# A self-scheduled recurrence-and-MLP kernel: new step durations, a reordered weight conversion, and a buffer left free earlier

## The chip, the cores and the metric

The kernel runs on one core of a Trainium2 chip. The metric is the device time of one execution in microseconds (us). Before the change it is 795.39 us, the median of three runs (794.29 to 796.77). The profile used below is of an execution of 794.98 us, whose recorded span is 793.3 us.

The engines have short names here: PE is the matrix engine (PEld its weight loads), DVE the vector engine, ACT the scalar (activation) engine, POOL the GpSimd engine. SP is the sync engine, which only issues transfers. POOL issues transfers too.

## The reference

A gated linear recurrence over time with a complex gate, followed by a two-layer MLP with a squared ReLU. Sizes: 4 batches, 8 heads, 768 time steps, head dimension 48; the MLP is 384 to 2048 to 384 over 3072 rows. The two MLP weights come as 64-bit floats.

```python
def _attn_ref(q, k, v, a_re, a_im):
    mag = np.sqrt(a_re * a_re + a_im * a_im)
    scale = np.minimum(mag, 0.999) / (mag + 1e-06)
    a_re_n, a_im_n = (a_re * scale, a_im * scale)
    ...
    for t in range(S):
        new_re = ar * S_re - ai * S_im
        new_im = ar * S_im + ai * S_re
        S_re, S_im = (new_re + kv, new_im)          # kv: outer product of k[t] and v[t]
        y[:, :, t] = np.einsum('bhd,bhde->bhe', q[:, :, t], S_re)

def _moe_ref(x, w_in, w_out):                       # x: the y of all heads side by side
    h = x @ w_in
    r = np.maximum(h, 0.0)
    return ((r * r) @ w_out).astype(np.float32)
```

## The kernel before

The time axis is cut into halves of 384 steps, which gives 8 units n = 0 to 7 (4 batches, two halves). A unit goes through three parts:

1. **The chain**, on DVE and ACT, for two groups of four heads (z = 0, 1): load `a` (the gate), q, k and v; normalise the gate (steps `sq`, `m2`, `ln`, `ex`, `s2`, `r1`, `r2`, `n1`, `n2`, `l1`, `l2`); multiply three neighbouring time steps together (`in10` to `in23`); invert the product (`iq`, `ia`, `il`, `ie`, `i1`, `i2`); transpose the ends on PE (`tot`); run a prefix product over time in ten parts on DVE (`scan`, eight tiny instructions in a part); transpose back (`bk`, copied to `xn`). Then the products `f` of `a` and `xn` are combined and applied to q and k (`QK`).
2. **The attention of four head pairs**, on PE with evictions on ACT and DVE: transposes `tq`, scores `sa`, states `kv` (from `KC`, the keys sent through DRAM as `rows` and read back), the mix `ypair`, the copy `yt`, and a transfer into `xT`.
3. **The dense part**: 16 pieces of `h` (three matmuls each), ReLU and square on ACT, then 3 output blocks `o` of 16 matmuls. Both together are 96 matmul instructions of 384 columns; as each fp32 matmul shows as two records, they are 192 records.

Nothing is placed by hand. Each piece of work is a `step` with an engine, a duration (`cost`, ns), a latency to its result (`lag`), a rank and its dependencies. `lay_out` plays the steps through with these numbers, and the order in which they start there is the order in which each engine gets its instructions. The real engines then work through these fixed queues and wait, in order, on semaphores. So a number in `step` changes no instruction; it changes the order.

```python
def lay_out():
    ...
    while ready:
        # for each engine: the steps that can start earliest, by rank among those nearly as early
        picks = [min((p for p in ps if p[0] <= min(ps)[0] + NEARLY.get(engine, 0)), key=lambda p: p[1])
                 for engine, ps in picks.items()]
        t, _, key = min(picks)
        engine, cost, lag, _, _, _, bank, until = steps[key]
        free[engine] = t + cost
        done[key] = t + cost + lag
        ...
    return [(t, key) for t, _, key in sorted(starts)]
```

The weights: 32 pieces (16 of each matrix) are fetched as 64-bit words and turned into fp32 in one ACT pass (`lower`) and three DVE passes that depend on each other.

```python
def lower(i):
    act.activation(out=lo, in_=lo, func=AF.Copy, scale=2.0 ** -29)

def convert(i, part):
    if part == 0:
        dve.tensor_scalar(out=bits, in0=hi, ...)                     # L676
    elif part == 1:
        dve.scalar_tensor_tensor(out=bits, in0=hi, ..., in1=bits, ...)   # L679
    else:
        dve.tensor_tensor(out=bits, in0=bits, in1=more, op=ALU.add)  # L683
```

`rest` is a check on the size of the inputs: ACT squares a tile into a scrap tile `junk` and keeps only the sum, for q, k and v.

```python
def measure(j, t):
    act.activation(out=junk[:, 0:t.shape[1]], in_=t, func=AF.Square, saturate=False,
                   accum_out=sums[:, n, j:j + 1])
...
for i in range(3):
    add(("rest", n, i), "ACT", act_cost(2 * NEL) + 90,
        [("kk", n, i) if i < 2 else ("v", n, W - 1)],
        lambda i=i: measure(4 + i, whole(u["qk", i]) if i < 2 else v_of_the_unit))   # v: cut
```

The last stage of the chain. In units 0 and 1 the two products are joined by PE into PSUM (`join_pe`, tile `P`); from unit 2 on by DVE (`join`), which writes into `a`:

```python
def cross(z, j, r):
    dve.tensor_tensor(out=u["fb" if j else "fa", z][:, r], in0=u["a", z][:, r], in1=over(z, j), op=ALU.mult)

def join(z, r):
    a, fa, fb = u["a", z], u["fa", z], u["fb", z]
    dve.tensor_tensor(out=flat(a[:, r]), in0=flat(fa[:, r]), in1=flat(fb[:, 1 - r]),
                      op=ALU.add if r else ALU.subtract)

def apply(z, j, r, i=None):
    p = u["a", z][:, r] if i is None else u["P", z, r, i]
    dve.tensor_tensor(out=outs(z)[j][...], in0=u["qk", z][:, j, hi], in1=p, op=ALU.mult)
```

There is one buffer `a` for each z, so the next unit's load of `a` waits until the last reader of the present one is through.

Of the kernel before, what the change touches and what calls it, by code (L numbers as in the profile page):

```python
# [481 lines left out]
def fast_path(ctx, tc, q, k, v, a_re, a_im, moe_w_in, moe_w_out, out, flag):  # L482
# [10 lines left out]
    nc = tc.nc  # L493
# [5 lines left out]
    NP = H // 2  # L499
# [185 lines left out]
    def weight_steps():  # L685
        for i in range(2 * NF):
            if i < FIRST:
                deps = [("gate", z) for z in range(2)]
            elif i < NF:
                deps = [("cv", i - FIRST, 2)]  # L690
            else:
                deps = [("cv", i - (NF - NF // 2 if i < NF + NRAW else NRAW), 2)]
            step(("fetch", i), "SP" if i >= NF else "POOL", 100 if i >= NF else 750, 400 + i,
                 deps, lambda i=i: fetch(i), 7000)
            rank = CONV[i // NF] + i
            step(("lower", i), "ACT", 470, rank, [("fetch", i), ("e2", 0, 1)], lambda i=i: lower(i))
            for part, cost in enumerate((270, 470, 470)):
                step(("cv", i, part), "DVE", cost, rank,
                     [("cv", i, part - 1), ("lower", i) if part == 2 else ("fetch", i),
                      ("ap", 0, 1)],  # L700
                     lambda i=i, part=part: convert(i, part))
# [41 lines left out]
    def chain_steps(u):  # L743
        n = u["n"]
        NEL = HH * W * D
        count = [0]
        get, queue, issue = ((nc.sync, "SP", 100) if n < 2 else (nc.gpsimd, "POOL", 750))

# [22 lines left out]
        for name in ("a", "qk"):  # L771
            for z in range(2):
                for j in range(2):
                    add(("ld", n, name, z, j), queue, issue,
                        [("ap", n - 1, z)],
                        lambda name=name, z=z, j=j: load(name, z, j),
                        lag=(4300 + 2700 * z if name == "a" else 8000) if n == 0 else 6000)
        for j in range(W):
            add(("v", n, j), queue, issue,
                [("mix", n - 2, NP - 1), ("kv", n - 2, NP - 1), ("rest", n - 2, 2)],  # L780
                lambda j=j: load_v(j), lag=9000 if n < 2 else 6000)
        if n == 0:
# [239 lines left out]
        for i in range(3):  # L1022
            add(("rest", n, i), "ACT", act_cost(2 * NEL) + 90,
                [("kk", n, i) if i < 2 else ("v", n, W - 1)],
                lambda i=i: measure(4 + i, whole(u["qk", i]) if i < 2 else
                                    u["v"].rearrange("p j h d -> p (j h d)")))

# [40 lines left out]
        def join(z, r):  # L1068
            a, fa, fb = u["a", z], u["fa", z], u["fb", z]
            dve.tensor_tensor(out=flat(a[:, r]), in0=flat(fa[:, r]), in1=flat(fb[:, 1 - r]),  # L1070
                              op=ALU.add if r else ALU.subtract)
# [9 lines left out]
        def apply(z, j, r, i=None):  # L1081
            hi = slice(0, HH) if i is None else ts(i, HH // 2)
            p = u["a", z][:, r] if i is None else u["P", z, r, i]
            dve.tensor_tensor(out=outs(z)[j][:, hi, :, r * D:(r + 1) * D],  # L1084
                              in0=u["qk", z][:, j, hi], in1=p, op=ALU.mult)
# [15 lines left out]
        for z in range(2):  # L1101
# [10 lines left out]
            for r in range(2):  # L1112
# [10 lines left out]
                else:  # L1123
                    add(("join", n, z, r), "DVE", D1, made + [("f", n, z, 1, r), ("f", n, z, 0, 1 - r)],
                        lambda z=z, r=r: join(z, r))
# [19 lines left out]
    def pair_steps(u, i):  # L1145
# [107 lines left out]
        for h in range(2):  # L1253
            step(("sa", n, i, h), "PE", 650, rank + 3 + 3 * h,
                 [("T", n, i, c) for c in range(W)] + free, lambda h=h: score(h),
                 bank="sc", until=("A", n, i, h))
            step(("A", n, i, h), "DVE", 480, -20, [("sa", n, i, h)],
                 lambda h=h: scored(h))
        step(("kv", n, i), "PE", 165 * chunks, rank + 4,
             [("KC", n, z), ("v", n, W - 1), ("mix", n - 1, NP - 1)] + free, keep, bank=bank(True), until=("S", n, i, chunks - 1))  # L1260
        for j in range(chunks):
            step(("S", n, i, j), "DVE", 180, -21,
                 [("kv", n, i), ("S", n, i, j - 1)],
                 lambda j=j: kept(j))
        step(("mix", n, i), "PE", 1300 if late else 1100, rank + 12,
             [("A", n, i, h) for h in range(2)] + [("S", n, i, chunks - 1), was("y", 1)], mix)
        step(("y", n, i), "ACT", 400, -25, [("mix", n, i), was("xT", 2)], mixed)
        step(("xT", n, i), "SP", 200, -25, [("y", n, i), ("h", n - 2, NF - 1)], place, lag=2400)


    def dense_steps(u):
# [44 lines left out]
        for c in range(W):  # L1316
            for p in range(4):
# [103 lines left out]
```

## Time and profile before

| What | Value |
|---|---|
| time, median of 3 | 795.39 us |
| span of the profiled execution | 793.3 us |
| PE busy | 712.3 us, 90% |
| DVE busy | 509.7 us, 64% |
| ACT busy | 411.4 us, 52% |
| POOL busy | 107.1 us, 14% |
| dense matmuls, 1536 records of 487 to 496 ns | about 517 us of the PE time |
| mean granted PE clock | 0.979 |

A row of the wait table reads: engine, what waited (tile and line), what it waited for, then the total in us, how many times, and the longest. A row of the timeline reads: start in us, length in us, engine, line, operation, output and inputs, shape, number of instructions merged into the row, and in brackets the idle time ahead of it with what ended it. A row of the window table reads: the stretch in us, its length, the busy time of each engine in it (with its number of instructions), the PE clock as a share of full speed, the share of the transfer engines, and GB/s. Matmul records overlap, so a single record's length is more than the distance to the next: 24 dense records take 7.74 us on the chain of waits, 0.3225 us each, which is 0.645 us for one instruction.

### The profile page before, as it was taken

What the parts mean: (1) busy time and instruction counts of PE and PEld (TensorE: products, weight loads), DVE (VectorE), ACT (ScalarE), POOL (GpSimd) and SP (SyncE); (2) the same over time, 40 slices, a digit from 0 to 9 for tenths busy, and PEclk for the clock granted to TensorE, in tenths of its full rate; (3) what the DMA queues carried; (4) which work ended last, traced back from release to release, by engine and by line L of the source; (5) the groups of instructions that cost most, each with busy time, mean ns of one, the idle gap of its engine ahead of it and who ended that gap; (6) DMA issues with size and microseconds to landing.
All of it is one profiled execution on the core that took longest, in us unless ns stands there. A gap on an engine that the chain in (4) does not pass through costs nothing.

```text
span 793.3 us, 9897 instructions
## 1 busy us (share of the span) xinstructions
PE 712.3 (90%) x3538; PEld 474.7 (60%) x3538; DVE 509.7 (64%) x1184; ACT 411.4 (52%) x754; POOL 107.1 (14%) x157
## 2 busy tenths in 40 slices
PE   0139789989699999999999999999999999999996
PEld 0018645658466775776586668656865775555553
DVE  5498778886769679767966794698659536610000
ACT  5445359507493766775387538754775233502510
POOL 5001200004102210400121030103000204300000
PEclk9999789989899999999999999999999999999999
DMA  9406464007202520611161043105200518800000
GB/s 283 153 1 217 122 204 134 19 12 228 52 1 76 181 63 11 219 26 55 67 197 45 11 151 104 46 0 196 91 14 0 190 35 283 288 12 22 0 11 23
DMA packets 39068, 76.25 MB, mean 96 GB/s; under 512 B 10753, under 2 KB 25217, under 8 KB 39009
## 3 DMA queue, kind: packets, MB, share of 16 engines
q0 software_dynamic: 14208, 53.88, 21.1%
q1 hardware_dynamic: 24800, 21.64, 9.0%
q8 instruction: 30, 0.49, 0.3%
q14 instruction: 30, 0.24, 0.1%
HBM read 56.62 MB, written 14.16 MB: 89 GB/s over the span
## 4 chain that ended last, share of the span: by engine, by line
PE 68%; DVE 19%; ACT 4%; SPq 3%; DMA 3%; issue 2%; ACTq 0%; DVEq 0%
PE h L1277 24%; PE o L1294 22%; PE sa L1183 5%; PE tq L1170 5%; DVE fa L980 5%; PE kv L1197 4%; PE ypair L1219 3%; DVE e L987 2%; SPq L768 2%; PE ypair L1224 2%; PE P L1078 2%; ACT fa L806 2%; DVE qk L852 1%; DVE fa L985 1%; DMA xT<-yt 1%
## 5 line engine op out<-in xcount | busy, mean ns | idle before, releaser
L1277 PE MATMUL h<-xT,w 128*128 128x384 f32 x768 | 261.6, 496 | 8.5 <-DMA xT<-yt 8.4
L1294 PE MATMUL o<-w,g 128*128 128x384 f32 x768 | 255.5, 487 | 0.0
L1277 PEld LDWEIGHTS h<-xT,w 128*128 128x128 f32 x768 | 146.1, 194 | 106.5 <-issue 16.4
L1294 PEld LDWEIGHTS o<-w,g 128*128 128x128 f32 x768 | 143.0, 190 | 92.0 <-issue 0.6
L1175 ACT COPY QKT<-tq 96x512 f32<-96x512 f32 x96 | 76.3, 868 | 67.1 <-PE tq L1170 66.4
L1284 ACT ACTIVATE g<-h 128x384 f32<-128x384 f32 x128 | 62.4, 487 | 89.9 <-PE h L1277 89.5
L1287 ACT ACTIVATE g<-g 128x384 f32<-128x384 f32 x128 | 67.1, 524 | 3.5
L1299 ACT COPY ot<-o 128x384 f32<-128x384 f32 x24 | 11.5, 480 | 102.7 <-PE o L1294 101.2
L1091 POOL DMA_DIRECT2D rows<-QK x16 | 9.1, 571 | 386.1 <-DVE QK L1084 386.1
L1189 DVE TENSOR_TENSOR A<-sa,mask 128x384 f32<-128x384 f32 x64 | 35.1, 554 | 35.7 <-PE sa L1183 34.1
L1183 PE MATMUL sa<-QKT 96*128 96x128 f32 x384 | 52.7, 281 | 2.8 <-ACT QKT L1175 2.2
L803 DVE TENSOR_TENSOR fb<-fa 128x576 f32<-128x576 f32 x32 | 24.2, 755 | 43.2 <-ACT fa L901 25.1
L1183 PEld LDWEIGHTS sa<-QKT 96*128 96x128 f32 x384 | 47.0, 191 | 7.9 <-ACT QKT L1175 2.7
L1170 PE MATMUL tq<-ident,QK 128*96 128x128 f32 x384 | 51.1, 273 | 0.4 <-DVE QK L1084 0.4
L980 DVE TENSOR_TENSOR fa<-e 128x192 f32<-128x192 f32 (+6 forms) x152 | 48.2, 358 | 2.0
L1170 PEld LDWEIGHTS tq<-ident,QK 128*96 128x96 f32 x384 | 42.7, 127 | 11.1 <-issue 8.2
L933 PE MATMUL tot<-ident,last 128*128 128x128 f32 x72 | 12.0, 294 | 37.7 <-ACT last L859 33.8
L806 ACT ACTIVATE fa<-fb 128x576 f32<-128x576 f32 x64 | 41.6, 675 | 7.0 <-DVE fb L803 5.1
L1219 PE MATMUL ypair<-A,v 128*48 128x128 f32 x384 | 37.2, 287 | 1.2 <-ACT yt L1229 1.2
L1197 PE MATMUL kv<-v,KC 128*96 128x48 f32 x320 | 32.9, 254 | 2.9 <-DMA KC<-rows 2.9
L1197 PEld LDWEIGHTS kv<-v,KC 128*96 128x96 f32 x320 | 31.2, 171 | 6.5 <-DMA KC<-rows 3.8
L933 PEld LDWEIGHTS tot<-ident,last 128*128 128x128 f32 x72 | 9.4, 149 | 42.9 <-issue 35.2
(105 smaller groups left out, 855.9 us busy)
## 6 DMA issues: line engine op xcount, KB each, us to landing
rows<-QK POOLq DMA_DIRECT2D x16, 576.0 KB, 3.6
raw<-in_moe_w_in_dram POOLq DMA_DIRECT2D x16, 384.0 KB, 7.7
raw<-in_moe_w_out_dram SPq DMA_DIRECT2D x16, 384.0 KB, 3.7
look<-in_moe_w_in_dram POOLq DMA_DIRECT2D x16, 384.0 KB, 5.2
look<-in_moe_w_out_dram POOLq DMA_DIRECT2D x16, 384.0 KB, 4.0
KC<-rows POOLq DMA_DIRECT2D x8, 576.0 KB, 5.8
out_dram<-ot SPq DMA_DIRECT2D x24, 192.0 KB, 1.9
xT<-yt SPq DMA_DIRECT2D x48, 72.0 KB, 2.3
```

The source lines that it names most:

```text
L806: act.activation(out=parts(z)[dst], in_=parts(z)[src], func=func, **kw)
L980: dve.tensor_tensor(out=t, in0=x, in1=y[:, j].unsqueeze(1).to_broadcast(shape), op=ALU.mult)
L1170: nc.tensor.transpose(ps[:, 2 * j + h], src, ident)
L1175: act.copy(out=u["T", i].rearrange("r z (p c) -> r c z p", c=W)[:, c], in_=u["tq", i, c])
L1183: nc.tensor.matmul(sa[:, j], lhsT=T[:, 2 + h, ts(j, C)], rhs=T[:, h, ts(j, C)], start=True, stop=True)
L1189: dve.tensor_tensor(out=u["A", i][:, h], in0=u["sa", i, h], in1=mask3, op=ALU.mult)
L1197: nc.tensor.matmul(ps[:, j, h], lhsT=u["KC", hh // HH][:, j, hh % HH], rhs=u["v"][:, j, hh], start=True, stop=True)
L1219: nc.tensor.matmul(ypair[64 * h:64 * h + D, ts(j, C)], lhsT=u["v"][:, j, 2 * i + h], rhs=A[:, h, j], start=True, stop=S_j is None)
L1277: nc.tensor.matmul(ps, lhsT=w1[:, f, m], rhs=u["xT"][:, m], start=(m == 0), stop=(m == NM - 1))
L1284: act.activation(out=t, in_=u["h", f], func=AF.Relu)
L1287: act.activation(out=u["g", f], in_=u["g", f], func=AF.Square)
L1294: nc.tensor.matmul(u["o", c], lhsT=u["g", f][:, ts(c, C)], rhs=w2[:, f], start=(f == 0), stop=(f == NF - 1))
```

## The change

It has five parts. None adds or takes away an arithmetic instruction.

- **Durations**: the issue of a transfer on SP is now planned with 500 to 600 ns (before 100 to 200), a `kv` product with 330 (165), the scores `sa` with 740 (650), the mix with 1230 or 1420 (1100 or 1300), and some load latencies are new. This is to bring the planned order nearer to what the engines do.
- **The sum of squares of v last**: it gets a late rank, and the planned landing of unit 0's v is put at 27 us in place of 9.
- **The conversion in pairs**: the rank of the DVE passes is made so that two pieces go through in turn (first pass of both, second pass of both, third pass of both), where before one piece went through all three.
- **The products of the last stage leave `a`**: `join` writes into `fa`, not `a`. `a` is then free as soon as the four `f` products are made, and the loads of the next `a` are planned from there.
- **Dependencies that follow from this**: `join` needs two products only; unit 1's v load is planned after unit 0's inversion.

```diff
-            step(("fetch", i), "SP" if i >= NF else "POOL", 100 if i >= NF else 750, 400 + i,
+            step(("fetch", i), "SP" if i >= NF else "POOL", 600 if i >= NF else 750, 400 + i,
...
-                step(("cv", i, part), "DVE", cost, rank,
+                step(("cv", i, part), "DVE", cost, CONV[i // NF] + i // 2 * 6 + part * 2 + i % 2,
...
-                        [("ap", n - 1, z)],
+                        [("f", n - 1, z, i, r) for i in range(2) for r in range(2)]
+                        if name == "a" else [("ap", n - 1, z)],
                         lambda name=name, z=z, j=j: load(name, z, j),
-                        lag=(4300 + 2700 * z if name == "a" else 8000) if n == 0 else 6000)
+                        lag=(3300 + 1500 * z if name == "a" else 8000) if n == 0 else 6000)
...
-                [("mix", n - 2, NP - 1), ("kv", n - 2, NP - 1), ("rest", n - 2, 2)],
-                lambda j=j: load_v(j), lag=9000 if n < 2 else 6000)
+                [("mix", n - 2, NP - 1), ("kv", n - 2, NP - 1), ("rest", n - 2, 2)]
+                + ([("e2", 0, 1)] if n == 1 else []),
+                lambda j=j: load_v(j), lag=27000 if n == 0 else 8000)
...
-                                    u["v"].rearrange("p j h d -> p (j h d)")))
+                                    u["v"].rearrange("p j h d -> p (j h d)")),
+                rank=1000 * n + 900 if i == 2 else None)
...
-            a, fa, fb = u["a", z], u["fa", z], u["fb", z]
-            dve.tensor_tensor(out=flat(a[:, r]), in0=flat(fa[:, r]), in1=flat(fb[:, 1 - r]),
+            fa, fb = u["fa", z], u["fb", z]
+            dve.tensor_tensor(out=flat(fa[:, r]), in0=flat(fa[:, r]), in1=flat(fb[:, 1 - r]),
...
-            p = u["a", z][:, r] if i is None else u["P", z, r, i]
+            p = u["fa", z][:, r] if i is None else u["P", z, r, i]
...
-                    add(("join", n, z, r), "DVE", D1, made + [("f", n, z, 1, r), ("f", n, z, 0, 1 - r)],
+                    add(("join", n, z, r), "DVE", D1, made,
...
-            step(("sa", n, i, h), "PE", 650, rank + 3 + 3 * h,
+            step(("sa", n, i, h), "PE", 740, rank + 3 + 3 * h,
...
-        step(("kv", n, i), "PE", 165 * chunks, rank + 4,
+        step(("kv", n, i), "PE", 330 * chunks, rank + 4,
...
-        step(("mix", n, i), "PE", 1300 if late else 1100, rank + 12,
+        step(("mix", n, i), "PE", 1420 if late else 1230, rank + 12,
...
-        step(("xT", n, i), "SP", 200, -25, ..., place, lag=2400)
+        step(("xT", n, i), "SP", 600 * (3 if i % 4 in (1, 2) else 2), -25, ..., place, lag=2400)
...
-            step(("out", n, c), "SP", 100, -15, [("ot", n, c)], lambda c=c: store(c), lag=2500)
+            step(("out", n, c), "SP", 500, -15, [("ot", n, c)], lambda c=c: store(c), lag=2500)
```

(The issue of the first two units' loads on SP goes from 100 to 600 in the same way.)

More of the change, by code (lines that the diff above doesn't have):

```diff
@@ L746, in chain_steps @@
         count = [0]
-        get, queue, issue = ((nc.sync, "SP", 100) if n < 2 else (nc.gpsimd, "POOL", 750))
+        get, queue, issue = ((nc.sync, "SP", 600) if n < 2 else (nc.gpsimd, "POOL", 750))
         def add(key, engine, cost, deps, fn, rank=None, **kw):
@@ L1264, in pair_steps @@
                  lambda j=j: kept(j))
-        step(("mix", n, i), "PE", 1300 if late else 1100, rank + 12,
+        step(("mix", n, i), "PE", 1420 if late else 1230, rank + 12,
              [("A", n, i, h) for h in range(2)] + [("S", n, i, chunks - 1), was("y", 1)], mix)
         step(("y", n, i), "ACT", 400, -25, [("mix", n, i), was("xT", 2)], mixed)
-        step(("xT", n, i), "SP", 200, -25, [("y", n, i), ("h", n - 2, NF - 1)], place, lag=2400)
+        step(("xT", n, i), "SP", 600 * (3 if i % 4 in (1, 2) else 2), -25, [("y", n, i), ("h", n - 2, NF - 1)], place, lag=2400)
     def dense_steps(u):
```

## The prediction

> **What bounds the kernel now.** I read the busy shares first: PE is busy for 712.3 of 793.3 us. An order can't shorten that work, so what can be won is PE's idle time, 793.3 − 712.3 = 81.0 us, and the time in which PE runs at a lower clock. The next view is the table of what PE waited for, over the whole span:
>
> ```profile
> PE tot L933 <- ACT last L859: 33.8, 1, 33.8
> PE bk L933 <- DVE e L987: 18.6, 6, 11.7
> PE h L1277 <- DMA xT<-yt: 8.4, 2, 4.5
> PE tot L933 <- ACT last L861: 3.9, 2, 3.7
> PE kv L1197 <- DMA KC<-rows: 2.9, 2, 2.1
> ```
>
> Nearly all is the first chain, before PE has anything to do (33.8, 3.7 and 11.7 us). Of the other 18.6 − 11.7 = 6.9 us for `bk`, 2.45 come in unit 1 and the rest in four waits of at most 1.8 us. Then the windows of 20 us say where the rest lies and where the clock is low:
>
> ```profile
> 80.00:100.00 20.00, 14.28 (x98) 11.59 (x96) 15.81 (x39) 5.64 (x10) 4.27 (x5) 0.74 0.45 126
> 100.00:120.00 20.00, 17.90 (x47) 10.33 (x48) 15.35 (x32) 11.46 (x24) 0.00 (x0) 0.83 0.61 207
> ...
> 160.00:180.00 20.00, 16.55 (x60) 10.76 (x59) 17.97 (x53) 2.69 (x6) 0.77 (x2) 0.83 0.03 10
> 180.00:200.00 20.00, 18.39 (x165) 15.96 (x163) 12.12 (x29) 15.25 (x24) 7.73 (x11) 1.00 0.73 232
> 200.00:220.00 20.00, 14.33 (x85) 9.14 (x86) 13.87 (x29) 9.75 (x19) 2.66 (x3) 0.83 0.18 45
> ```
>
> The first number after the length is PE. Idle: 5.7, 2.1, 3.4, 1.6 and 5.7 us; from 220 us to the end of the matmuls only about 4.6 us in all. So there are three places: the start, the attention of units 0 and 1, and the seam at 167 to 178 us between unit 0's dense part and unit 1's attention.
>
> **The start, read from ACT's timeline.**
>
> ```profile
> 15.63 0.67 ACT L820 ACTIVATE junk<-fb 128x576 fp8e5<-128x576 f32 x1
> 16.20 0.18 ACT L820 ACTIVATION_READ_ACCUMULATOR junk<-fb 128x1 f32 x1
> 27.90 1.16 ACT L820 ACTIVATE junk<-v 128x1152 fp8e5<-128x1152 f32 x1 [11.51 <-DMA v<-in_v_dram]
> 28.96 0.19 ACT L820 ACTIVATION_READ_ACCUMULATOR junk<-v 128x1 f32 x1
> 29.93 1.16 ACT L820 ACTIVATE junk<-v 128x1152 fp8e5<-128x1152 f32 x1 [0.78 <-DMA v<-in_v_dram]
> 31.00 0.19 ACT L820 ACTIVATION_READ_ACCUMULATOR junk<-v 128x1 f32 x1
> 31.09 2.20 ACT L901 ACTIVATE fa<-a 128x1152 f32<-128x1152 f32 x2
> ```
>
> ACT stands still for 11.5 us because two sums of squares of v are next in its queue and v hasn't landed. L901 (`iq`), the next link of the chain, stands behind them. On DVE its input is made by this row, and DVE then has nothing until 32.27 us:
>
> ```profile
> 23.86 0.62 DVE L847 TENSOR_TENSOR a<-fa 128x192 f32<-128x192 f32 x2
> ```
>
> The first of the two (z = 0) is done at 23.86 + 0.35 = 24.2 us.
>
> **The seam, read from PE's timeline.**
>
> ```profile
> 161.84 5.33 PE L1294 MATMUL o<-w,g 128*128 128x384 f32 x16
> 169.61 1.54 PE L933 MATMUL bk<-ident,e 128*128 128x128 f32 x6 [2.45 <-DVE e L987]
> 171.97 1.33 PE L1078 MATMUL P<-fa,ident 128*128 128x288 f32 x2 [0.82 <-DVE fa L1065]
> ```
>
> Dense 0 ends at 167, unit 1's prefix product on DVE ends at 169.8. DVE is busy for 15.4 to 18.0 us of each 20 us from 80 to 180 us (77 to 90%), much of it with the 32 weight pieces, so in this stretch DVE sets when unit 1 can begin.
>
> [...] in 2 us windows the clock is 0.50 from 170 to 176 and from 212 to 216 us, each after a gap. So a gap costs more than its length. [...] two independent passes of 0.55 us (the masks `A`) take 1.01 us, so the second starts 0.46 us after the first; in a dependent weight piece the second pass starts 0.39 and the third 0.69 us later. [...] transfers issued by SP and POOL share the 16 engines. The trace shows their share at about 1.0 from 98 to 106 us, when the last `xT` of unit 0 took 5.0 us against a median of 2.3.
>
> **The change part by part.** I compared the orders in which the two programs' instructions stand on each engine; they hold no times.
>
> *v last.* On ACT the two `junk<-v` move from ahead of `iq` to behind the `lower` passes, just ahead of unit 0's last `xn` copies, where ACT was idle for 6.76 us; they need 2 × 1.26 = 2.5 us and fit, and v is there by 30 us. DVE's and PE's order in the first chain is unchanged. `iq` starts at 24.2 in place of 31.09 us: **−6.9 us**, all on the path, as everything up to the first `P` hangs on this chain.
>
> *Conversion in pairs.* One piece alone takes 1.45 us while it waits for nothing (0.38 + 0.60 + 0.47) and 1.56 (0.39 + 0.69 + 0.48) later. In pairs each pass costs its independent distance: 0.27 (two 0.35 us operations take 0.62) + 0.47 + 0.47 = 1.21 us. In the new order the 16 pieces of the first matrix and about 8 of the second go in pairs: 24 × about 0.28 = 6.5 us less DVE time. The first `lower` of the second matrix comes one ReLU earlier on ACT; the DVE waits for it (2.23, 1.08, 0.18 and 1.02, together 4.5 us) should shrink. Two chain passes of unit 1 (`r1`, `r2`, 1.4 us) move into unit 0's attention. That makes unit 1's chain some 8 to 12 us earlier against the dense part. It has to be: in the new order `bk` of the complex part stands after 40 of the 48 `o` instructions, 8 × 0.645 = 5.2 us ahead of where dense 0 ends. As 8 is more than 5.2 + 2.45, I expect no wait there. Won: the idle 2.45 + 0.82 = 3.3 us, `bk` warm (0.97 in place of 1.54), and eight `P` warm (two groups of 1.94 us as in unit 0, 3.9, in place of 6.4 from 171.97 to 178.4): 3.3 + 0.6 + 2.5 = 6.4. Something is lost again since `P` still waits for DVE's `f`: I take **−5.5 us**.
>
> *Unit 0's attention.* `r1` and `r2` of unit 1 now stand between the `QK` of z = 1, and ACT squares unit 1's second `a` ahead of the first `yt`. Both delay `rows`, `KC` and `yt` by about 0.7 to 0.8 us (one or two passes of 0.75 us). One weight fetch stands ahead of the last `xT` on SP, and its 384 KB share the transfer engines. I take **+0.8 us**. The waits for `KC` (2.1) and `xT` (3.8) stay.
>
> *Unit 1's attention.* Unit 2's loads of `a` for both z now stand ahead of `rows` on POOL (four issues of 0.75 us), so `KC` may land up to 2 us later; it had come just in time. ACT has unit 2's `iq` ahead of the first ReLUs, and PE stops for unit 2's `tot` after 3 `h`, where before 15 stood ahead. The wait for `xT` of 4.5 us stays. I take **+0.5 us**.
>
> *`a` free earlier, and the durations, from unit 2 on.* The load of `a` starts earlier by two `join` and four `QK`, 6 × 0.67 = 4 us. ACT waited for `a` 4.4 us in all, 3.3 of them in the first unit, so it is nearly hidden, and PE had 4.6 us of idle time to give. A better plan may take some of it; a plan that puts `bk` earlier may add some: **−0.5 us**.
>
> Sum: −6.9 − 5.5 + 0.8 + 0.5 − 0.5 = −11.6 us; 795.4 − 11.6 = 783.8 us.
>
> **The rivals.** (a) *Only the start pays.* DVE's gain is eaten by waits for ACT, which now has unit 1's chain between its ReLUs, and `bk` stops PE in the middle of dense 0 rather than at its end. For it: DVE's queue is in order, and its longest waits in this stretch were for ACT. Against it: 8 to 12 us of relief for 7.7 needed. It gives about 788 to 789. (b) *More is won.* If the keys come back 2 us sooner in unit 0, PE stays warm from 88 to 97 us, where it ran at 0.50, and some 4 us more go; together with the idle time from unit 2 on that is about 777. Against it: the order of POOL there is the same, with two weight fetches ahead of `KC`. (c) *Transfers become the wait.* Unit 2's `a` ahead of `rows`, and a weight fetch ahead of `xT`, each add 2 to 3 us and a cold stretch: 789 to 791. For it: the transfer share is near 1.0 in four of the eight 2 us windows from 182 to 198 us. (d) *The new order is worse for PE from unit 2 on*: `bk` waits grow from 1 to 2 us to 3 in six units, +6: about 790. Against it: the new PE durations are nearer to the profile (the `kv` of a pair with three blocks takes 1.0 to 1.15 us on the chain of waits, where 3 × 165 ns were planned).
>
> **Range and chances.** The start is nearly sure. The seam is worth 3 to 7; the attention of units 0 and 1 costs −1 to +4; the rest lies between −3 and +4. I take 778 to 789.5 us. Two per cent is 779.5, which needs rival (b) in part: 0.15. Slower by 2% would need all of (c) and (d) and more: 0.01.
>
> **What would show it.** Right: the first `P` on PE at about 50 us rather than 56.9, with no wait of ACT for v; the seam without a `bk` wait and with the clock at 1.0; weight pieces at 1.2 us; PE idle about 68 us in all rather than 81. Wrong: an ACT wait in the start that takes v's place, a `bk` or `tot` wait inside dense 0 or 1, `KC` waits above 3 us, or a row of PE waits after 220 us of more than 8 us together.

## The result and the profile after

The changed kernel takes 776.87 us (median of 4 runs, 774.88 to 778.07) against 795.12 us before: a ratio of 0.9765, 95% interval 0.9739 to 0.9792. A second measurement gave 777.83 us and 0.9780 (0.9756 to 0.9803). I had predicted 783.8 us and a range from 778.0 to 789.5. The direction was right; the gain is 18 us where I had 11.6, and the time lies just below the range.

The profiled execution has a span of 776.3 us against 793.3. First the busy line of the page (busy time and share of the span for each engine), then the table of what PE waited for (total, times, longest), both of the changed kernel:

```profile
PE 709.7 (91%) x3538; PEld 474.8 (61%) x3538; DVE 503.3 (65%) x1184; ACT 409.8 (53%) x754; POOL 107.2 (14%) x157
```

```profile
PE tot L935 <- ACT last L861: 27.3, 1, 27.3
PE bk L935 <- DVE e L989: 14.0, 6, 11.7
PE h L1280 <- DMA xT<-yt: 6.5, 2, 3.6
PE tot L935 <- ACT last L863: 3.9, 2, 3.7
PE kv L1200 <- DMA KC<-rows: 2.9, 2, 2.3
```

PE's idle time fell from 81.0 to 776.3 − 709.7 = 66.6 us, and its busy time by 2.6 us, although it executes the same 3538 records: I read those 2.6 us as time at the lower clock (its mean over the span is 0.984, before 0.979). The first wait is 6.5 us shorter. Of the waits for `bk` beyond the 11.7 us of the first unit, 2.3 us are left of 6.9. The wait for `KC` is the same.

The windows of 20 us of the changed kernel (PE busy first; third number from the right the clock):

```profile
80.00:100.00 20.00, 15.46 (x75) 11.11 (x76) 15.32 (x39) 3.53 (x7) 2.68 (x3) 0.59 0.49 150
100.00:120.00 20.00, 20.00 (x63) 11.79 (x63) 18.07 (x37) 17.92 (x37) 0.00 (x0) 1.00 0.58 187
...
160.00:180.00 20.00, 19.20 (x134) 15.18 (x132) 14.61 (x32) 12.52 (x20) 8.46 (x12) 1.00 0.68 212
180.00:200.00 20.00, 15.07 (x137) 12.46 (x138) 16.62 (x33) 13.54 (x25) 2.66 (x3) 0.89 0.27 75
200.00:220.00 20.00, 19.65 (x65) 11.50 (x65) 18.25 (x61) 14.71 (x31) 0.00 (x0) 0.94 0.00 0
```

The seam between unit 0's dense part and unit 1's attention now lies at 155 to 167 us; in the window from 160 us PE is busy for 19.20 us at a clock of 1.00, where before it was 16.55 at 0.83. The attention of unit 0 is the bad place that stayed: a clock of 0.59 from 80 to 100 us.

Two timelines carry the rest. On ACT of the changed kernel, L903 (the square `iq`) waits for its own input only, and not for v:

```profile
24.51 2.22 ACT L903 ACTIVATE fa<-a 128x1152 f32<-128x1152 f32 x2 [7.86 <-DVE a L849]
```

On PE of the changed kernel, the seam (start, length, operation; a wait would stand in brackets):

```profile
146.99 7.91 PE L1297 MATMUL o<-w,g 128*128 128x384 f32 x24
154.96 0.97 PE L935 MATMUL bk<-ident,e 128*128 128x128 f32 x6
155.77 2.75 PE L1297 MATMUL o<-w,g 128*128 128x384 f32 x8
158.35 0.65 PE L1081 MATMUL P<-fa,ident 128*128 128x288 f32 x2
```

There is no bracket at `bk`, and it runs at the full clock (1.00 from 154 to 160 us; 0.97 us for six, before 1.54). `o` matmuls of the dense part stand between `bk` and `P`, and again between the fourth and the fifth `P`, so PE has work while DVE makes the `f` products.

On DVE of the changed kernel, two weight pieces in turn:

```profile
86.29 0.62 DVE L676 TENSOR_SCALAR w<-raw 128x384 uint32<-128x384 uint32 x2
86.83 1.02 DVE L679 SCALAR_TENSOR_TENSOR w<-raw,w 128x384 uint32<-128x384 uint32 x2
87.76 1.02 DVE L683 CUSTOM_DVE_ANT_0 w<-raw,w 128x768 uint16<-128x768 uint16 x2
88.70 0.62 DVE L676 TENSOR_SCALAR w<-raw 128x384 uint32<-128x384 uint32 x2
```

From 86.29 to 88.70 us it takes 2.41 us for two pieces, 1.21 us for one.

### The profile page after: what moved, and what is told of

Same layout as the page of the kernel before. It is cut to its first block, busy times and chain, and to the rows that moved or that the text cites. A ratio compares the mean times of both kernels' runs of the same rounds, so it can differ in the third digit from the quotient of the medians.

```text
span 776.3 us, 9918 instructions
## 1 busy us (share of the span) xinstructions
PE 709.7 (91%) x3538; PEld 474.8 (61%) x3538; DVE 503.3 (65%) x1184; ACT 409.8 (53%) x754; POOL 107.2 (14%) x157
## 4 chain that ended last, share of the span: by engine, by line
PE 68%; DVE 21%; ACT 3%; DMA 3%; issue 2%; SPq 0%; POOL 0%; ACTq 0%; DVEq 0%
PE h L1280 24%; PE o L1297 23%; DVE fa L982 5%; PE sa L1186 5%; PE tq L1173 4%; PE kv L1200 3%; PE ypair L1222 3%; DVE e L989 3%; PE P L1081 2%; PE ypair L1227 2%; DMA KC<-rows 2%; DVE fa L987 1%; ACT fa L808 1%; DVE e L990 1%; DMA xT<-yt 1%
## 5 line engine op out<-in xcount | busy, mean ns | idle before, releaser
L1297 PEld LDWEIGHTS o<-w,g 128*128 128x128 f32 x768 | 143.5, 190 | 94.1 <-issue 0.7
L762 POOL DMA_DIRECT2D a<-in_a_re_dram x12 | 9.0, 753 | 209.3 <-issue 99.3
L1087 DVE TENSOR_TENSOR QK<-qk,fa 128x576 f32<-128x576 f32 x48 | 33.1, 755 | 0.0
```

The costliest lines, as they stand in the source:

```text
L1297: nc.tensor.matmul(u["o", c], lhsT=u["g", f][:, ts(c, C)], rhs=w2[:, f], start=(f == 0), stop=(f == NF - 1))
```

## The experiments

Each run changes either the kernel before or the changed kernel. Its median is set against runs of the kernel before on the same chip at the same time; "worth" below is the ratio's distance from 1 times 795 us.

Two marks cut the span of each profile in three, so that a gain can be placed: the first `P` on PE, and **h1**, the moment at which unit 1's dense part goes on after its wait for `xT`. The last column is PE's idle time from 222 to 700 us, which is 478 less PE's busy time in that window.

| Kernel | median us | ratio (95%) | first P | first P to h1 | h1 to end | span | idle 222-700 |
|---|---|---|---|---|---|---|---|
| before | 794.4 to 795.1 | 1 | 56.9 | 155.0 | 581.4 | 793.3 | 4.6 |
| v last, alone (e5) | 787.80 | 0.9906 (0.9872-0.9941) | 49.8 | 155.6 | 581.2 | 786.6 | 4.8 |
| pairs alone (e6) | 791.97 | 0.9965 (0.9950-0.9980) | 56.7 | 146.9 | 582.2 | 785.8 | 6.2 |
| pairs alone again (e15) | 790.62 | 0.9968 (0.9939-0.9997) | 56.7 | 148.5 | 583.8 | 789.0 | 6.3 |
| durations alone (e7) | 792.50 | 0.9975 (0.9959-0.9992) | 56.8 | 149.0 | 584.0 | 789.8 | 7.3 |
| a's part alone (e13) | 788.50 | 0.9918 (0.9896-0.9939) | 57.0 | 153.9 | 577.3 | 788.3 | 2.8 |
| changed (first profile, e8) | 776.87, 777.83 | 0.9765, 0.9780 | 50.4, 49.5 | 146.6, 147.1 | 579.3, 579.5 | 776.3, 776.1 | 2.9, 3.0 |
| changed without v last (e14) | 784.48 | 0.9873 (0.9846-0.9901) | 56.6 | 145.2 | 580.3 | 782.0 | 3.9 |
| changed without pairs (e2) | 783.90 | 0.9844 (0.9805-0.9883) | 49.9 | 149.4 | 584.8 | 784.1 | 7.0 |
| changed without durations (e3) | 782.61 | 0.9832 (0.9794-0.9870) | 50.2 | 151.4 | 582.3 | 784.0 | 8.3 |
| changed without a's part (e4, e12) | 781.60, 779.90 | 0.9828 (0.9788-0.9867), 0.9811 (0.9787-0.9834) | 50.2, 49.6 | 146.8, 145.5 | 580.6, 583.0 | 777.6, 778.1 | 5.1, 5.7 |

My theory, as the prediction has it: the start and the pairs make the time, the durations and `a` hardly count. The rivals: the new durations move unit 1's chain and make the seam; or `a`'s part does more than hide a wait.

### The start

**e1**: the kernel before with two edits.

```diff
-                lambda j=j: load_v(j), lag=9000 if n < 2 else 6000)
+                lambda j=j: load_v(j), lag=27000 if n == 0 else 9000 if n < 2 else 6000)
...
-                                    u["v"].rearrange("p j h d -> p (j h d)")))
+                                    u["v"].rearrange("p j h d -> p (j h d)")),
+                rank=1000 * n + 900 if i == 2 else None)
```

> The kernel before, with one part of the change: the sum of squares of v gets the late rank and v's planned landing is 27 us. All else is as before. If this part is worth what the start shows (first P at 56.9 us before, 50.4 after): first P near 50.4 us, seam and attention of unit 1 unchanged, 795.1 - 6.6 = 788.5 us. Rival: the start is only lent, since DVE with its weight pieces sets the pace up to the seam; then the wait for bk in unit 1 grows from 2.45 us and the time is 790 to 793.

Measured: 794.37 us, ratio 0.9992 (0.9980 to 1.0004), and the first `P` at 56.9 us. Neither theory fits. ACT's timeline of this run says why:

```profile
29.85 1.17 ACT L820 ACTIVATE junk<-v 128x1152 fp8e5<-128x1152 f32 x1 [13.70 <-DMA v<-in_v_dram]
30.92 0.19 ACT L820 ACTIVATION_READ_ACCUMULATOR junk<-v 128x1 f32 x1
31.02 2.20 ACT L901 ACTIVATE fa<-a 128x1152 f32<-128x1152 f32 x2
```

One sum of v still stands ahead of L901. The two sums there belong to units 0 and 1, and I had moved unit 0's only: unit 1's v was still planned to land early. Moving one of two blockers is worth nothing; ACT waits for the other. What I had put aside as a dependency that follows from the change, unit 1's v load planned after unit 0's inversion, is half of this part.

**e5**: the same with that edit.

```diff
-                [("mix", n - 2, NP - 1), ("kv", n - 2, NP - 1), ("rest", n - 2, 2)],
-                lambda j=j: load_v(j), lag=9000 if n < 2 else 6000)
+                [("mix", n - 2, NP - 1), ("kv", n - 2, NP - 1), ("rest", n - 2, 2)]
+                + ([("e2", 0, 1)] if n == 1 else []),
+                lambda j=j: load_v(j), lag=27000 if n == 0 else 8000)
```

> The kernel before, with all three edits that put the sum of squares of v last: the late rank, the planned landing of unit 0's v at 27 us, and unit 1's v load planned after unit 0's inversion (in the run with only the first two, the sum of unit 1's v still stood ahead of L901 and held ACT until 31.0 us). If the start is worth what it shows: L901 at 24.5 us, first P at 50.4 us, all later marks of PE 6.6 us earlier, 788.5 us. Rival: the start is only lent, as the three DVE passes of the weights are not faster; then the wait for bk in unit 1 grows from 2.45 us and the time is 790 to 793 us.

Measured: 787.80 us, a worth of 7.5 us. ACT's timeline of this run:

```profile
23.92 2.22 ACT L902 ACTIVATE fa<-a 128x1152 f32<-128x1152 f32 x2 [7.86 <-DVE a L848]
```

The first `P` is 7.1 us earlier in its profile and nothing else moved (155.6 and 581.2 in the table, with the wait of 2.47 us for `bk` in unit 1 as before). The start is not lent.

**e14**, the opposite: the changed kernel with the three edits of e5 undone.

> The changed kernel with the sums of squares of v in their old place and the old plan for v's loads. If the start is worth the same with the other parts as alone (7.1 us): L901 at 31 us again, first P near 57 us, 783.5 to 785.5 us. If the parts share a gain (a later start would be hidden behind waits further on): 780 to 783 us.

Measured: 784.48 us, 0.9873 against 0.9780, so 7.4 us lost. The first `P` is at 56.6 us, and both later stretches are within 1 to 2 us of the changed kernel's. The part is worth the same in both companies.

### The pairs and the durations

**e2**: the changed kernel with the old rank of the conversion.

```diff
-                step(("cv", i, part), "DVE", cost, CONV[i // NF] + i // 2 * 6 + part * 2 + i % 2,
+                step(("cv", i, part), "DVE", cost, rank,
```

> The changed kernel with the weight conversion piece by piece again (old rank of the three passes). Theory 1, that the pairs free DVE and so give the 9 us between the restart of dense 0 and that of unit 1: a wait for bk comes back in unit 1, 782 to 786 us. Theory 2, that the new durations do it by placing unit 1's chain earlier: 777 to 778.5 us, no wait for bk.

Measured: 783.90 us. A wait for `bk` is back in unit 1 (PE's timeline of this run):

```profile
159.18 0.97 PE L935 MATMUL bk<-ident,e 128*128 128x128 f32 x6 [1.18 <-DVE e L989]
```

But it costs 1.2 us, not 6. In the table only 2.3 to 2.7 us are lost between the first `P` and h1, and 5.4 after it, where PE's idle time is 7.0 us rather than 2.9.

**e3**: the changed kernel with the old durations and landing times of `a` (of eight lines, the three on PE are shown; the other five are SP's issues and `a`'s landing).

```diff
-            step(("sa", n, i, h), "PE", 740, rank + 3 + 3 * h,
+            step(("sa", n, i, h), "PE", 650, rank + 3 + 3 * h,
...
-        step(("kv", n, i), "PE", 330 * chunks, rank + 4,
+        step(("kv", n, i), "PE", 165 * chunks, rank + 4,
...
-        step(("mix", n, i), "PE", 1420 if late else 1230, rank + 12,
+        step(("mix", n, i), "PE", 1300 if late else 1100, rank + 12,
```

> The changed kernel with the old durations of SP issues, kv, scores, mix and the old landing times of a; v last, pairs and the free a stay. Theory 1 (pairs): 777 to 778.5 us. Theory 2 (durations): the seam and unit 1's attention lose most of their 9 us, 782 to 786 us.

Measured: 782.61 us, against theory 1. Of the 4.6 us ahead of h1 more than half stand in unit 0's attention, where PE stood still for 4.5 us in front of an `h`; the profile names no releaser for that wait. Behind h1 it loses 3 us; the waits of PE from 212 to 640 us in this run:

```profile
PE bk L935 <- DVE e L989: 5.1, 4, 1.7
PE kv L1200 <- DMA KC<-rows: 2.8, 3, 1.6
```

**e6** and **e15**: the kernel before with the pairs alone (the diff of e2 the other way round), twice.

> The kernel before, with the conversion in pairs and nothing else. The start stays (first P 56.9 us). If the pairs by themselves free DVE: from the restart of dense 0 to that of unit 1 about 103 to 105 us in place of 109.8, 789 to 791 us. If pairs pay only with the new durations: 793 to 796 us.

> The kernel before with the conversion in pairs, a second profile. If the first profile (787.5 us) was only a lucky one: 791 to 795 us, first P to restart of dense 1 at 147 to 152 us, the difference somewhere in waits for transfers. If the profile is typical and the median was not: 787 to 789 us.

Measured: 791.97 and 790.62 us, a worth of 2.5 to 2.8 us. The profiles show 6.5 to 8.1 us won between the first `P` and h1, and 0.9 to 2.4 lost behind it. The first profile is of a quick execution of this kernel (787.5 us; 19 runs lie between 787.5 and 795.5), the second is nearer to its median. A single profile places a gain; only the median sizes it.

**e7**: the kernel before with the durations alone.

> The kernel before, with the new durations and landing times and nothing else. The wait for v in the start stays or moves. From the two runs that leave out pairs and durations I expect the two not to add up: the durations alone save 3 to 6 us between the restart of dense 0 and that of unit 1 (bk of the complex part then stands after dense 0), 789 to 793 us. Rival: as the order from unit 2 on is a matter of luck, the rest may give or take 5 us: 786 to 797 us.

Measured: 792.50 us, a worth of 2.0 us: 6 us won ahead of h1, 2.7 lost behind it, with 7.3 us of idle time from 222 to 700 us. So pairs and durations both move unit 1's chain, and share one gain: alone 8.1 (or 6.5) and 6.0 us ahead of h1, together 8 us. Where neither has `a`'s part beside it, both lose some of it in the later units.

### a's part

**e4** and **e12**: the changed kernel with `join` writing into `a`, and the old dependencies of `a`'s loads and of `join`.

```diff
-                        [("f", n - 1, z, i, r) for i in range(2) for r in range(2)]
-                        if name == "a" else [("ap", n - 1, z)],
+                        [("ap", n - 1, z)],
...
-            dve.tensor_tensor(out=flat(fa[:, r]), in0=flat(fa[:, r]), in1=flat(fb[:, 1 - r]),
+            dve.tensor_tensor(out=flat(a[:, r]), in0=flat(fa[:, r]), in1=flat(fb[:, 1 - r]),
```

> The changed kernel with join writing into a again and a's loads waiting for the last reader, as before. As I worked it out, a leaving early hides at most a few tenths of a us of ACT's wait: 776.5 to 777.5 us. Rival: the 2.0 us won from unit 2 on come from the earlier a: about 779 us.

> The changed kernel with join writing into a again, a second time with more rounds, as its first four times (779.4 to 783.2 us) and its profiled span (777.6 us) did not say the same. If a's part is worth nothing: 776.5 to 778.5 us. If it is worth what the first median says: 781 to 782 us.

Measured: 781.60 and 779.90 us, 0.9828 and 0.9811 against 0.9780 for the changed kernel: 2.5 to 3.8 us lost, more than the tenths I had counted. The intervals overlap with that of the changed kernel, but eight of the nine runs without `a`'s part (778.58 to 783.16 us) lie above all nine with it (774.88 to 778.71). Nothing is lost ahead of h1.

**e13**: the kernel before with `a`'s part alone (the diff of e4 the other way round).

> The kernel before, with join writing into fa, a's loads planned from the four f products, and join's shorter list of dependencies; nothing else. If a's part pays by itself, as ACT waits 4.4 us for a: 792 to 793.5 us. If it is hidden, and only pays where the other parts have made the chain of the later units the bound: 794.5 to 796 us.

Measured: 788.50 us, a worth of 6.5 us, better than the best that I had written down. The window from 222 to 700 us of this run, and PE's wait for `bk` in it:

```profile
222.00:700.00 478.00, 475.25 (x2503) 320.52 (x2502) 331.42 (x770) 268.24 (x492) 76.94 (x109) 1.00 0.30 98
```

```profile
PE bk L934 <- DVE e L988: 1.4, 2, 1.2
```

PE is idle for 478 − 475.25 = 2.75 us there, against 4.58 in the kernel before.

**e17** separates its two sides. Leaving `a` frees the buffer (a real wait), and it changes a dependency that `lay_out` reads (the plan). This run has the first without the second: every engine's instructions stand as in the kernel before.

```diff
-            dve.tensor_tensor(out=flat(a[:, r]), in0=flat(fa[:, r]), in1=flat(fb[:, 1 - r]),
+            dve.tensor_tensor(out=flat(fa[:, r]), in0=flat(fa[:, r]), in1=flat(fb[:, 1 - r]),
...
-            p = u["a", z][:, r] if i is None else u["P", z, r, i]
+            p = u["fa", z][:, r] if i is None else u["P", z, r, i]
```

> The kernel before, with join writing into fa and the products read from there, but the planned dependencies as before: the same order on every engine, and the loads of a are issued where they stood. If the 6 us of a's part come from a's real wait (the load could start up to 4 us earlier): 789 to 792 us. If they come from the new order that the plan makes of it: 794 to 795.5 us.

Measured: 794.54 us, ratio 1.0000 (0.9984 to 1.0017). The wait for `bk` from 222 to 700 us is that of the kernel before (4.5 us in 4, the longest 1.8):

```profile
PE bk L933 <- DVE e L987: 4.6, 4, 1.8
```

In the old order the free buffer is worth nothing. But it could hardly be used there: POOL's queue has the load of `a` behind `rows`, which waits for the last `QK`. POOL's timeline of e17, then of e13:

```profile
250.04 0.57 POOL L1091 DMA_DIRECT2D rows<-QK  x1 [42.41 <-DVE QK L1084]
250.60 0.75 POOL L762 DMA_DIRECT2D a<-in_a_re_dram  x1
```

```profile
234.10 0.76 POOL L762 DMA_DIRECT2D a<-in_a_re_dram  x1 [24.83 <-ACT g L1285]
```

The last `f` product ends at 247.07 us in e17 and at 233.55 us in e13. So the load still starts 3.5 us after it in e17 (4.7 in the kernel before), and 0.55 us after it in e13, where the new plan puts the loads of `a` ahead of `rows` and orders PE, ACT and DVE anew. What `a`'s part wins comes with the plan. How much of it is the earlier load and how much the new order of the other engines was not separated, nor was the plan tried without the buffer. ACT's own wait for `a` is small: from 180 to 700 us it is 1.1 us in the kernel before and none in e13.

**e8** is the changed kernel again, as a measure:

> The changed kernel once more, beside the parts on the same chip: 776 to 778 us, as its first measurement. It is the measure for the leave-one-out runs.

Measured: 777.83 us. The four parts alone multiply to 0.9906 × 0.9965 × 0.9975 × 0.9918 = 0.9766; the change as a whole measured 0.9765 and 0.9780. The intervals of the four, put together by squares, leave 0.5% (4 us) to either side, so the parts add up as far as this can tell, and an overlap of a few us is not excluded: the profiles show one ahead of h1. Leaving one part out gives other numbers: v costs 7.4 us (alone 7.5), the pairs 5.1 (2.7), the durations 4.1 (2.0), `a` 2.5 to 3.8 (6.5), the difference of the ratios to 0.9780 times 795 us, with some 3 us of uncertainty each. So for no single part do the medians show that the two numbers differ; what the parts share is seen in the profiles alone.

### What the low clock costs

Rival (b) of the prediction hung on the clock of 0.50 in unit 0's attention, which the change left. Four runs fill PE's waits with idle products (ident by ident, written into a tile that the next real product overwrites), on top of the changed kernel; none of the kernel's own work is left out.

**e10**: right ahead of the `kv` that waits for `KC`, and ahead of the first `h` of units 0 and 1 (four records of that `h` still run before its wait for `xT`).

```diff
             ps = u["kv", i] = tile([R, NM, 2, D], "kv", True)
+            for j in range(12 if n == 0 and i == 2 else 0):
+                nc.tensor.matmul(ps[:, 0].rearrange("p h d -> p (h d)"), lhsT=ident[:, 0:R],
+                                 rhs=ident[:, 0:2 * D], start=True, stop=True)
...
             ps = u["h", f] = dp.tile([C, L], F32, name="h", tag="d")
+            for m in range(12 if n < 2 and f == 0 else 0):
+                nc.tensor.matmul(ps[:, 0:C], lhsT=ident, rhs=ident, start=True, stop=True)
```

> The changed kernel with 12 idle products of 96 columns ahead of the kv of unit 0 that waits 2.3 us for KC, and 12 of 128 columns ahead of the first h of units 0 and 1, which wait 3.0 to 3.6 us for xT. If the clock of 0.50 from 80 to 93 us, at 96 to 100 us and after unit 1's xT comes from these waits, it goes: kv in 2.2 us in place of 4.1, ypair at half its time, 24 records of h in 7.7 us in place of 9.3 to 11: 770 to 773 us. Rival: the idle products delay what follows, or xT does not land sooner: 777 to 779 us.

Measured: 773.20 us, 0.9727 (0.9701 to 0.9754). First the product that waits for `KC` in PE's timeline of the changed kernel, then the same place in e10:

```profile
80.97 4.07 PE L1200 MATMUL kv<-v,KC 128*96 128x48 f32 x24 [2.28 <-DMA KC<-rows]
```

```profile
77.77 2.20 PE L1198 MATMUL kv<-ident 128*96 128x96 f32 x24
80.22 2.24 PE L1203 MATMUL kv<-v,KC 128*96 128x48 f32 x24 [0.25 <-DMA KC<-rows]
```

The idle products take the 2.2 us that PE would have stood, and the 24 records behind them take 2.24 us in place of 4.07. The clock is 1.00 from 78 to 84 us, where it was 0.88, 0.50 and 0.50. The cold stretch after unit 1's wait is gone as well (1.00 from 192 to 200 us, where the wait is 0.84 us and not 3.57); the one after unit 0's `xT` is not (0.65 and 0.50 from 92 to 96 us), and a wait of 2.62 us is left there. From the first `P` to h1 it takes 143.5 us in place of 146.6. Part of the gain is lost again: unit 2's `bk` now waits 2.0 us for DVE at 212.9 us (0.35 before).

**e9**: 40 idle products in the first chain, where PE waits 11.7 us for unit 0's prefix product; **e11**: both.

```diff
+            for m in range(40 if n == 0 and name == "bk0" else 0):
+                nc.tensor.matmul(u[name][:, 0], lhsT=ident, rhs=ident, start=True, stop=True)
             for m in range(NM):
                 nc.tensor.transpose(u[name][:, m], src(m), ident)
```

> The changed kernel with 40 idle products (ident by ident, 128 columns, into the buffer of unit 0's bk, overwritten by it) in PE's wait of 11.7 us for the prefix product. If the low clock is what makes the first P products take 0.97 us a pair in place of 0.49, they run warm and the first tq starts up to 2.3 us sooner: about 775 us. Rival: DVE, which makes fa and fb and reads P, sets the pace there, and nothing is won: 777 to 778 us.

> Both of the last two together. If both gains are real and add up: 767 to 771 us, faster than either kernel. If the clock is not at fault: 777 to 779 us.

Measured: 778.86 us for e9, which is no gain, and 774.62 us for e11, no better than e10. PE's timeline of e9:

```profile
35.68 10.70 PE L935 MATMUL bk<-ident 128*128 128x128 f32 x80
47.73 0.97 PE L937 MATMUL bk<-ident,e 128*128 128x128 f32 x6 [1.34 <-DVE e L991]
50.56 1.33 PE L1083 MATMUL P<-fa,ident 128*128 128x288 f32 x2 [1.86 <-DVE fa L1070]
51.68 1.16 PE L1083 MATMUL P<-fb,minus 128*128 128x288 f32 x2
```

`bk` ran warm (0.97 us for six, 1.54 in the changed kernel), `P` did not: about 0.96 us from one to the next, as without the idle products. Between the last idle product and the first `P` lie 1.34 us of waiting, 0.97 us of transposes and 1.86 us of waiting. DVE was not the brake, as only the first `P` waits.

**e16**: e11 with eight more idle products right ahead of the first `P`.

```diff
+            for _ in range(8 if n == 0 and (z, r, i) == (0, 0, 0) else 0):
+                nc.tensor.matmul(ps.rearrange("p h c d -> p (h c d)")[:, 0:C], lhsT=ident,
+                                 rhs=ident, start=True, stop=True)
             for f, w, start in ((u["fa", z][:, r], ident, True),
```

> The kernel with all idle products, and 8 more of 128 columns right ahead of the first P. In the two runs with idle products in the first chain, bk ran at 0.97 us but P at 0.96 us a pair, as if nothing had been done: between the last idle product and the first P lie 1.2 us idle, 0.97 us of transposes and 1.9 us idle. [...] the eight products keep it up: P at 0.49 us a pair, first tq up to 2.3 us sooner, 771 to 773 us. If DVE sets the pace, P waits for DVE instead and the time stays 773 to 775 us.

Measured: 771.89 us, 0.9718 (0.9689 to 0.9746), the lowest median of this study, 5 to 6 us below the changed kernel. Its interval overlaps with those of e10 and e11, so what it adds to them is read from the profile alone. PE's timeline of e16:

```profile
47.83 1.95 PE L1082 MATMUL P<-ident 128*128 128x128 f32 x16
49.86 0.75 PE L1086 MATMUL P<-fa,ident 128*128 128x288 f32 x2
50.53 0.75 PE L1086 MATMUL P<-fb,minus 128*128 128x288 f32 x2
51.12 0.65 PE L1086 MATMUL P<-fa,ident 128*128 128x288 f32 x2
```

The `P` products now stand 0.48 to 0.67 us apart (with one wait of 0.43 us for DVE after the fourth), and the first `tq` comes 28.3 us after the first `tot` in place of 29.9 in the changed kernel (54.90 − 26.64 and 57.13 − 27.27). The mean clock of the profile is 0.998 against 0.984, though the latter counts the cold `P` of the changed kernel as 1.00 (see the end). The time lies within the 771 to 773 us that I had written down for a warm `P`. The clock, which reads 0.82 from 48 to 50 us and 0.50 from 50 to 56 us in e9, is 1.00 over both stretches here.

## Why the prediction was off

Measured by its own terms, as distances between marks in the profiles. Both measured columns are of the changed kernel: the first is its first profile (the last column says how it is read), the second is e8. They sum to the 17.0 and 17.2 us by which the spans are shorter.

| Term | predicted | first profile | e8 | how the first is read |
|---|---|---|---|---|
| start | −6.9 | −6.6 | −7.4 | first `P` 56.93 → 50.37 |
| unit 0's attention | +0.8 | +0.6 | −0.5 | first `P` to `h` after `xT`: 45.17 → 45.78 |
| seam | −5.5 | −7.5 | −6.3 | `h` after `xT` to first `tq` of unit 1: 76.48 → 70.87, with four more `P` instructions (1.94 us) in it |
| unit 1's attention | +0.5 | −1.5 | −1.2 | first `tq` to h1: 33.36 → 29.96, without those four |
| from unit 2 on | −0.5 | −2.0 | −1.8 | h1 to end: 581.4 → 579.3 |

A term of a single profile is good to 1 or 2 us: the two columns differ by up to 1.3, and e17, with the order of the kernel before, has 74.9 us at the seam for that kernel's 76.5. What the profiles show beyond the 11.6 us comes in all of the last three terms: 0.8 to 2.0 us at the seam, 1.7 to 2.0 in unit 1's attention, 1.3 to 1.5 from unit 2 on. My range had room for each of them alone. With 6.9 us for the start, the good ends that I gave (7 for the seam, 1 for the two attentions, 3 for the rest) add up to 17.9 us, which is 777.5 us. I ended the range at 778, as if they would not meet; they did.

**Right.** The start: the size, that it lies on the path, and that nothing later takes it back (e5, e14). Unit 0's attention, within what a profile can tell. The weight pieces at 1.21 us, and PE's idle time of 66.6 us for the 68 that I named. The relief in front of the seam: unit 1's prefix product ends 104.9 us after the first `P` rather than 113.0, 8 us earlier and so at the lower end of my 8 to 12; against the 7.7 us needed, it was just enough, and `bk` starts without a wait. (24 × 0.28 us of DVE time is 6.7 and not the 6.5 that I wrote; DVE's busy time fell by 6.4.)

**The seam, mis-sized.** I had worked out 6.4 us and took 0.9 off again because `P` still waits for DVE's `f`. That deduction was wrong: in the new order `o` matmuls stand where PE would have waited, and neither profile has a wait at `P` there. The 6.3 us of e8 are the 6.4. The first profile has 1.2 us more, as its cold stretch after unit 0's `xT` ends earlier: the 92 records of `h` take 31.5 us there, 32.6 in the kernel before, and 32.8 in e8. So these 1.2 us are chance.

**Unit 1's attention, wrong in sign.** I had `KC` up to 2 us later behind unit 2's loads of `a`. No wait for `KC` shows up there; the wait for `xT` got shorter, 3.57 and 3.84 us in place of 4.53. By the same marks, where the kernel before takes 33.4 us, e6, e15 and e7 take 31.4, 31.5 and 32.4, and e13 33.7. So this gain comes with the pairs and the durations; by which wait is open.

**The step that failed: "`a` free earlier, and the durations, from unit 2 on".** I gave it −0.5 us, since ACT's wait for `a` is nearly hidden. Alone, the durations are worth 2.0 us and `a`'s part 6.5; without `a`'s part the changed kernel loses 2.5 to 3.8. That the wait is nearly hidden stands: 1.1 us of it lie between 180 and 700 us, and the free buffer in the old order wins nothing (e17). I then stopped, and did not ask what else the same line does. In this kernel a dependency is also an input to the planner, so an edit that removes a hidden wait can still move every later unit's chain. I had put PE's idle time from unit 2 on at 4.6 us and let a tenth of it go; with `a`'s part alone 2.75 us are left from 222 to 700 us, and without it, with pairs or durations alone, 6 to 7. Of the 4.0 us that e13 wins behind h1, 1.8 are this idle time and, by my estimate, 0.9 a shorter cold stretch after h1 (at 0.3225 us a record, the first 26 of `h` lose 2.65 of their 11.04 us in the kernel before, the first eight lose 1.75 of their 4.33 us in e13); about 1 us I can't assign.

**The pairs, right in place but not in worth.** Alone they win the seam (6.5 to 8 us ahead of h1) and give back a part of it later, so 2.5 to 2.8 us are left. The durations alone win nearly the same place. My attribution of the seam to the pairs alone was wrong: either of the two does most of it.

**The rivals.** (a) and (c) did not happen. (d), with `bk` waits of 3 us, did not happen in any run: from 222 to 700 us the longest is 1.9. More idle time there did, 1.6 to 3.7 us in e2, e3, e6, e15 and e7, partly in waits for `KC`, `yt` and `QK`. (b) had the right number, 777, by luck: its first half did not come true (the wait for `KC` in unit 0 is 2.28 us for 2.09, and the clock stayed at 0.50), and the gain came from unit 1 and the plan; only its second half, the idle time from unit 2 on, did. Its price for the cold stretch was fair: I had written some 4 us, and e10 wins 3 to 3.6 us up to h1 and 3.7 to 4.6 us in all.

## What to carry to other kernels

In a kernel that plans its own order, list for each edited line both what the engine will wait for and what the planner will read, and try the two apart; a hidden wait does not make the edit worthless. Measure a part both alone and by leaving it out, since parts may share a gain as pairs and durations do ahead of h1; let the profile place the gain and the median size it. And where PE must wait a few us in front of short products, the cold stretch behind the wait can cost more than the wait itself: behind a wait of 2.28 us, `kv` and `ypair` of unit 0 took 9.3 us, and 5.3 us when idle products filled that wait (e10).

## What was new about the hardware

- In these traces waits of 0.94 to 2.28 us came with a fall of the clock to 0.50. In the changed kernel PE waits 0.94 us ahead of the last `sa` of unit 0 and 2.28 us ahead of the `kv` behind it, and from 80 to 92 us the clock is 0.50; in e10, with idle products in place of the second wait, it is 1.00 from 76 to 92 us. Four stretches of 4 us, as rows of the window table: two of the changed kernel, then one each of e9 and e16.

```profile
76.00:78.00 2.00, 1.06 (x10) 0.92 (x9) 2.00 (x5) 1.43 (x2) 0.00 (x0) 1.00 0.96 275
78.00:80.00 2.00, 0.69 (x7) 0.50 (x5) 2.00 (x6) 0.55 (x1) 0.00 (x0) 0.88 0.99 365
...
178.00:180.00 2.00, 1.59 (x16) 1.26 (x12) 0.76 (x1) 1.97 (x4) 0.64 (x1) 1.00 0.88 244
180.00:182.00 2.00, 1.14 (x21) 1.14 (x22) 1.93 (x3) 2.00 (x5) 0.00 (x0) 1.00 0.39 156
```

```profile
46.00:48.00 2.00, 0.66 (x6) 0.47 (x5) 1.97 (x7) 0.00 (x0) 0.00 (x0) 1.00 0.00 0
48.00:50.00 2.00, 0.70 (x6) 0.35 (x4) 1.97 (x8) 0.90 (x2) 0.00 (x0) 0.82 0.00 0
```

```profile
46.00:48.00 2.00, 0.97 (x8) 0.87 (x9) 1.93 (x9) 0.39 (x1) 0.00 (x0) 1.00 0.00 0
48.00:50.00 2.00, 1.93 (x17) 1.73 (x17) 2.00 (x4) 0.51 (x2) 0.00 (x0) 1.00 0.03 8
```

  In the first and the third PE was busy for 1.75 and 1.36 of the 4 us, and the 2 us behind them read 0.50; in the second and the fourth it was busy for 2.73 and 2.90 us, and the 2 us behind them read 1.00. What decides it was not shown. The 80 records of idle products in e9 end 4.2 us ahead of the first `P`, and about 0.96 us lie between the next `P` products; with 16 more records directly ahead of the first, in e16, it is 0.48 to 0.67 us (those 16 alone were not tried).
- The clock column of the changed kernel reads 1.00 from 50 to 56 us, while `P` takes 0.96 us at a time, twice the 0.48 us of later. In e9, where the column had fallen to 0.82 from 48 to 50 us, the stretch from 50 to 56 us reads 0.50, with `P` at the same 0.96 us. So the 1.00 there could not be taken at its word, and I read the durations.
- In the weight conversion a DVE pass that reads what the pass just ahead of it wrote started later than one behind the other piece's pass. In a piece alone (the kernel before), where DVE did not wait for another engine in between, the second pass starts 0.38 to 0.41 us after the first, once 0.46, and the third 0.58 to 0.72 after the second; in pairs (the rows of the changed kernel from 86.29 us), where the other piece's pass comes next, it starts 0.27 us after a first pass and 0.47 after a second. Two pieces in turn take 2.41 us, which is 1.21 for one against 1.45 to 1.56 for a piece alone.
